# Two finished chunks copied out of their accumulator banks early, in a fused linear-attention and SoLU kernel

## The chip, the cores and the metric

The kernel runs on one core of a Trainium2 chip. The metric is the device time of one execution in microseconds (us). All data is float32 on the engines; the weights arrive as float64 and are converted on the chip. Five engines work in parallel, each through its own queue of instructions in order: TensorE (PE in the profile, with its weight loads as PEld), VectorE (DVE), ScalarE (ACT), GpSimd (POOL) and SyncE (SP), which here only issues DMAs. Matmul results land in PSUM banks, which the other engines read; a bank is written again only after its readers are done.

## The reference

The first half is a gated linear recurrence over 4 batches, 8 heads, 768 steps and a head dimension of 48. The second half takes its output, one row of 384 numbers for each of 3072 tokens, through a feed-forward block with a softmax-gated activation and a layer norm.

```python
for t in range(S):
    state = alpha[:, :, t, :, None] * state + einsum('bhd,bhde', k[:, :, t], v[:, :, t])
    y[:, :, t] = einsum('bhd,bhde->bhe', q[:, :, t], state)
x = y.transpose(0, 2, 1, 3).reshape(3072, 384)
h = x @ w_in                                  # 384 -> 1024
solu = h * softmax(h)
ln = (solu - mean(solu)) / sqrt(var(solu) + 1e-6) * g_ln
out = ln @ w_out                              # 1024 -> 384
```

## The kernel before

The 768 steps are cut into six groups of 128 steps. One group covers all four batches, so it makes four chunks of 128 tokens; chunk n belongs to group n // 4 and batch n % 4. The order of all work is written out by hand in `fast_path`: every engine gets its instructions in the order in which the code issues them.

Attention for a group g needs these steps. `alpha_T(g)` transposes the decay factors on DVE (L179 and L182, 128x1024 and 128x512) into the buffer `aT`, after GpSimd has cleared one column of it (L188). `scan_back` and `scan_on` run multiplicative scans over `aT` on DVE (L204). Keys and queries are scaled by the scans' results; for group 1 this is L762 and L783 on DVE, straight out of PSUM banks. `move_lasts` and `move_firsts` rearrange the queries by DMAs from SyncE's queue into `q64`, the first 2064 columns of a tile named `lot`. `decay(g)` multiplies the running state on GpSimd (L264). `scores(g, half)` computes key-query products on PE (L280) into the four banks a0 to a3, and `masked(half)` multiplies them by the causal mask on DVE (L291), four instructions of 128x512. `read_state` and `read_values` (L329) write the attention output into the same four banks, and ScalarE copies it to SBUF as `x` (L359).

The feed-forward of a group starts with eight up products (`up`, L390), each into one of two banks named h, followed by exp on ScalarE (L404), a product on DVE (L405) and a square on ScalarE (L406). `down(n, half)` accumulates chunk n's output in eight matmuls of 128x385 (L501); column 384 collects the sum that the mean needs. There are two banks for these results (`ps_o`), so chunk n + 2 writes where chunk n was. `finish(n)` turns the accumulated chunk into the output: three small steps on DVE (L519, L521, L524), for group 0 also a correction by the mean row over 128x384 (L528), a power on GpSimd (L532, called pow below), a scaling on ScalarE (L534) into `o_sb`, and a store from SyncE's queue (L535). `o_mean` and `o_sb` have two buffers each.

The change lies in the stretch in which the four chunks of group 0 are brought down while group 1's attention runs and group 2's begins. There the order of calls is: `down(0, 1)`, `mean(1)`, `alpha_over(1)` (a range test on ScalarE, L196), `load(alpha, an, 2)`, `load(q, qn, 2)`, `down(1, 1)`, `keys_back(1)` (transposes L299 and ScalarE copies L301, L306), a scan, `apart()` (ScalarE, L248), `move_lasts()`, `finish(0)`, two scans with their query products, `move_firsts()`, `down(2, 0)`, the first scores, `finish(1)`, `decay(1)`, `masked(0)`, `down(2, 1)`, the second scores, `masked(1)`, `finish(2)`, `alpha_T(2)`, and then `down(3, ...)`, the reads, `scan_back(2)`, `keys_T(2)`, `keys(2)` (GpSimd, L228) and `finish(3)`.

Of the kernel before, what the change touches and what calls it, by code (L numbers as in the profile page):

```python
# [9 lines left out]
FP = mybir.dt.float32  # L10
# [4 lines left out]
ALU = mybir.AluOpType  # L15
AX = mybir.AxisListType
P = 128
# [15 lines left out]
def fast_path(ctx, tc, q, k, v, alpha, moe_w_in, moe_w_out, moe_g_ln, out):  # L33
# [12 lines left out]
    nc = tc.nc  # L46
    B, H, S, D = q.shape
    NTOK, DM = out.shape
# [13 lines left out]
    def pool(name, bufs, **kw):  # L62
        return ctx.enter_context(tc.tile_pool(name=name, bufs=bufs, **kw))
# [3 lines left out]
    work = pool("work", 2)  # L67
# [20 lines left out]
    mean_sb = const.tile([P, DM], FP, name="mean_sb")  # L88
# [5 lines left out]
    sums = const.tile([P, N, 4], FP, name="sums")  # L94
# [14 lines left out]
    SW = P + 1  # L109
    lot = const.tile([P, 4 * 768], FP, name="lot")  # L110
# [16 lines left out]
    st = [dict() for _ in range(N)]  # L127
# [3 lines left out]
    def load(src, dst, g):  # L131
        t = slice(g * P, (g + 1) * P)
        for b in range(B):
            nc.sync.dma_start(
                out=dst[32 * b : 32 * b + 32].rearrange("t h u d -> t h (u d)"),
                in_=src[b, :, t, :].rearrange("h (t u) d -> t h (u d)", u=TQ),
            )
# [40 lines left out]
    def firsts(src, dst):  # L178
        nc.vector.transpose(out=dst.rearrange("p h (t u) -> p h u t", u=TQ), in_=src[:, :, :, 0:E0])  # L179

    def lasts(src, dst):
        nc.vector.transpose(  # L182
            out=dst.rearrange("p j (i t u) -> p u j i t", u=TQ, i=2),
            in_=src[:, :, :, E0:D].rearrange("p (j i) u d -> p u j i d", i=2),
        )

    def alpha_T(g):
        nc.gpsimd.memset(aT[:, :, 0:1], 0.0)  # L188
        firsts(an, aT[:, 0:H, 1:SW])
        lasts(an, aT[:, H:NB, 1:SW])  # L190

    def alpha_over(g):
        x = an.rearrange("p h u d -> p (h u d)")
        sq = one.tile([P, 768], FP, name="sq").bitcast(U8)[:, 0 : x.shape[1]]
        for i, sign in enumerate((1.0, -1.0)):
            nc.scalar.activation(  # L196
                out=sq, in_=x, func=AF.Relu, scale=sign, bias=mone, accum_out=over[:, g, i : i + 1]
            )
# [12 lines left out]
    def scan_on(g, i):  # L211
        part = slice(NP * i, NP * i + NP)
        s = seed[i % 2]
        if i == 2:
            nc.vector.tensor_copy(out=fend[:, g], in_=h4[:, :, 1])

        least = small.tile([P, NP, 1], FP, name="least")
        nc.vector.tensor_scalar(out=least, in0=h4[:, part, 1:2], scalar1=LEAST, scalar2=None, op0=ALU.max)  # L218
        nc.vector.reciprocal(out=s[:, :, 0:1], in_=least)
        scan(aT[:, part], aT[:, part], s, False)  # L220
# [9 lines left out]
    def move_lasts():  # L230

        for b in range(B):
            i, c = divmod(b, 2)
            for k in range(2):
                nc.sync.dma_start(out=q64[64 * i + E0 : 64 * i + 64, c, k::2], in_=qe[32 * b : 32 * b + 32])
# [32 lines left out]
    def quarter(b):  # L268
        return slice(32 * b, 32 * b + 32)

    def banks(name, shape, n=B):
        return [ps_a.tile([P] + shape, FP, tag=f"a{b}", name=f"{name}{b}") for b in range(n)]
# [15 lines left out]
    def masked(half, batches=range(B)):  # L288
        a = masks[half]
        for b in batches:  # L290
            nc.vector.tensor_tensor(  # L291
                out=sT[:, b, half * NP : half * NP + NP], in0=a[b], in1=mask[:, None, :].to_broadcast([P, NP, P]),
                op=ALU.mult,
            )

    def keys_back(g, t=None):
        t = t or banks("tp", [NP, P], 3)
        for j in range(NB):
            nc.tensor.transpose(out=t[j // NP][:, j % NP], in_=kT[:, j], identity=ident)  # L299
        for i in range(2):  # L300
            nc.scalar.copy(  # L301
                out=kg[:, :, NP * i : NP * i + NP, 0:E0].rearrange("p b j d -> p j b d"),
                in_=t[i].rearrange("p j (b d) -> p j b d", b=B),
            )
        for m in range(2):
            nc.scalar.copy(  # L306
                out=kg[:, :, m::2, E0 + E1 * m : D + E1 * m].rearrange("p b j d -> p j b d"),
                in_=t[2].rearrange("p j (b k d) -> p j b k d", b=B, k=2)[:, :, :, m],
            )
# [69 lines left out]
    def u_of(g, f):  # L379
        return slots[((0, 5, 4), (1, 2, 3))[g % 2][f // 3]][:, T4 * (f % 3) : T4 * (f % 3) + T4]  # L380
# [114 lines left out]
    def down(n, half, part=range(HF)):  # L495
        g, b = divmod(n, B)
        d = st[n]
        if half == 0 and 0 in part:
            d["o"] = ps_o.tile([P, 512], FP, tag="o", name="o")
        for f in (half * HF + i for i in part):  # L500
            nc.tensor.matmul(  # L501
                d["o"][:, 0 : DM + 1], lhsT=u_of(g, f)[:, b * P : b * P + P], rhs=w_out[:, f], start=(f == 0),
                stop=(f == FC - 1), skip_group_check=True,
            )

    def finish(n):
        g, b = divmod(n, B)
        d = st[n]
        s, o = sums[:, n], d["o"][:, 0:DM]
        t0 = b * S + g * P  # L510
        if g == G - 1:
            o_sb = work.tile([P, DM], FP, name="o_sb")
            r = gr[g]["r"][:, b : b + 1]
            nc.vector.tensor_scalar(out=o_sb[:, 0:P], in0=o[:, 0:P], scalar1=r, scalar2=None, op0=ALU.mult)  # L514
            nc.scalar.activation(out=o_sb[:, P:DM], in_=o[:, P:DM], func=AF.Copy, scale=r)  # L515
            nc.scalar.dma_start(out=out[t0 : t0 + P, :], in_=o_sb)
            d.clear()
            return
        nc.vector.tensor_copy(out=s[:, 0:1], in_=d["o"][:, DM : DM + 1])  # L519
        t = small.tile([P, 1], FP, name="t")  # L520
        nc.vector.scalar_tensor_tensor(  # L521
            out=t, in0=s[:, 0:1], scalar=-1.0 / DFF, in1=s[:, 0:1], op0=ALU.mult, op1=ALU.mult
        )
        nc.vector.tensor_tensor(out=s[:, 3:4], in0=t, in1=gr[g]["s"][:, b : b + 1], op=ALU.add)  # L524
        if g == 0:

            o = work.tile([P, DM], FP, name="o_mean")
            nc.vector.scalar_tensor_tensor(  # L528
                out=o, in0=mean_sb, scalar=s[:, 0:1], in1=d["o"][:, 0:DM], op0=ALU.mult, op1=ALU.add
            )  # L530
        r = small.tile([P, 1], FP, name="r")
        nc.gpsimd.tensor_tensor(out=r, in0=s[:, 3:4], in1=mhalf, op=ALU.pow)  # L532
        o_sb = work.tile([P, DM], FP, name="o_sb")
        nc.scalar.activation(out=o_sb, in_=o, func=AF.Copy, scale=r)  # L534
        nc.sync.dma_start(out=out[t0 : t0 + P, :], in_=o_sb)  # L535
        d.clear()
# [82 lines left out]
    def mean(half):  # L619


        m = ps_h.tile([P, 512], FP, tag="h", name="sums")[:, 0:DM]
        if half == 0:
            for f in range(FC):
                r = quarter(f % 4)
                nc.tensor.matmul(
                    m[r], lhsT=ones[:, 0:32], rhs=w_out[:, f, 0:DM], start=f < 4, stop=f >= FC - 4,
                    tile_position=(0, r.start), skip_group_check=True,
                )
            made["m"] = work.tile([P, DM], FP, name="o_mean")  # L630
            nc.scalar.mul(out=made["m"], in_=m, mul=-1.0 / (32 * DFF))
        else:
            nc.tensor.matmul(m, lhsT=ones, rhs=made["m"], start=True, stop=True)
            nc.scalar.copy(out=mean_sb, in_=m)
# [34 lines left out]
    def three(name, where):  # L669
        return [pool.tile([P, NP, P], FP, tag=tag, name=f"{name}{i}") for i, (pool, tag) in enumerate(where)]  # L670
# [18 lines left out]
    for i in (2, 0, 1):  # L689
        if i == 1:  # L690
# [3 lines left out]
            out=qe[:, :, 0:P] if i == 2 else qv[:, part, 0:P], in0=t[i], in1=aT[:, part, 1:SW], op=ALU.mult  # L694
# [68 lines left out]
    mean(0)  # L763
    down(0, 1)
    mean(1)
    alpha_over(1)
    load(alpha, an, 2)
    tq += three("tp_q2", [(ps_h, "h")])
    turned(qn, ends_q, tq, range(H, NB))
    load(q, qn, 2)  # L770
    down(1, 1)
    keys_back(1, three("tp", [(ps_a, "a2"), (ps_a, "a3"), (ps_h, "h")]))
    scan_on(1, 2)
    nc.vector.tensor_tensor(out=qe[:, :, 0:P], in0=tq[2], in1=aT[:, H:NB, 1:SW], op=ALU.mult)
    apart()
    ends_of_decay()
    move_lasts()
    finish(0)
    in_range(7)
    for i in range(2):  # L780
        scan_on(1, i)
# [2 lines left out]
    move_firsts()  # L784
    down(2, 0)
    scores(1, 0)
    finish(1)
    decay(1)
    masked(0)
    down(2, 1)  # L790
    scores(1, 1)
    masked(1)
    finish(2)
    alpha_T(2)
    down(3, 0)
    read_begin()
    read_state(0)
# [87 lines left out]
    for g in range(1, G + 1):  # L885
# [10 lines left out]
        for s in range(FC):  # L896
# [16 lines left out]
            if todo:  # L913
                n, half = todo.pop(0)
# [24 lines left out]
    def compare(out, x, bound, op):  # L939
# [6 lines left out]
        out=chunks[:, :, 2], in0=sums[:, :, 2], scalar=0.25, in1=sums[:, :, 3], op0=ALU.mult, op1=ALU.is_le  # L946
# [6 lines left out]
    else:  # L953
# [9 lines left out]
        out=bad, in0=all_ok[0:1, 0:1], scalar1=float(P * ends[-1]), scalar2=None, op0=ALU.is_lt  # L963
# [451 lines left out]
```

## Time and profile before

| what | value |
|---|---|
| median of 4 runs | 383.38 us (382.6 to 384.52) |
| the profiled execution | 382.77 us, its span 381.0 us |
| granted TensorE clock, mean of the span | 0.997 |
| PE busy | 363.2 us, 95% of the span |
| DVE busy | 250.9 us, 66% |
| ACT busy | 144.2 us, 38% |
| POOL busy | 112.0 us, 29% |
| between 80 and 120 us: PE busy | 36.81 of 40 us |
| between 80 and 120 us: DVE busy | 35.40 of 40 us |

All terms below are from the profiled execution, whose clock starts with the span. A row of the order of time gives the start, the length, the engine, the line, the operation, what it writes and reads, how many instructions are merged in it, and in brackets how long the engine stood idle before and who ended that.

### The profile page before, as it was taken

What the parts mean: (1) busy time and instruction counts of PE and PEld (TensorE: products, weight loads), DVE (VectorE), ACT (ScalarE), POOL (GpSimd) and SP (SyncE); (2) the same over time, 40 slices, a digit from 0 to 9 for tenths busy, and PEclk for the clock granted to TensorE, in tenths of its full rate; (3) what the DMA queues carried; (4) which work ended last, traced back from release to release, by engine and by line L of the source; (5) the groups of instructions that cost most, each with busy time, mean ns of one, the idle gap of its engine ahead of it and who ended that gap; (6) DMA issues with size and microseconds to landing.
All of it is one profiled execution on the core that took longest, in us unless ns stands there. A gap on an engine that the chain in (4) does not pass through costs nothing. (4 is left out here: it accounts for less than half of the span.)

```text
span 381.0 us, 10060 instructions
## 1 busy us (share of the span) xinstructions
PE 363.2 (95%) x4341; PEld 216.1 (57%) x4341; DVE 250.9 (66%) x413; ACT 144.2 (38%) x255; POOL 112.0 (29%) x122
## 2 busy tenths in 40 slices
PE   8789899988999999999999999999999999999994
PEld 8675335556754656555665555665556565555552
DVE  0999878996999779884665875666874414444500
ACT  2528566672155436143261152341241132322100
POOL 6000000000243990455210475111475211332200
PEclk9999999999999999999999999999999999999998
DMA  9992968139239612927042626004033000000011
GB/s 184 168 330 79 211 211 210 41 89 189 66 85 192 159 37 64 186 58 179 4 105 58 132 70 167 22 4 99 7 78 78 22 2 21 23 22 21 22 45 48
DMA packets 72438, 36.05 MB, mean 95 GB/s; under 512 B 48184, under 2 KB 69952, under 8 KB 72384
## 3 DMA queue, kind: packets, MB, share of 16 engines
q1 hardware_dynamic: 71360, 34.39, 38.4%
q10 hardware_dynamic: 1024, 0.92, 0.7%
q8 instruction: 36, 0.59, 0.7%
q14 instruction: 18, 0.15, 0.1%
HBM read 25.30 MB, written 4.72 MB: 79 GB/s over the span
## 5 line engine op out<-in xcount | busy, mean ns | idle before, releaser
L390 PE MATMUL h<-x,w_in 128*128 128x512 f32 x288 | 133.4, 601 | 3.9 <-DVE room L405 2.7
L501 PE MATMUL o<-w_out,room 128*128 128x385 f32 x384 | 133.6, 492 | 1.1 <-DVE least L218 1.1
L501 PEld LDWEIGHTS o<-w_out,room 128*128 128x128 f32 x384 | 71.1, 189 | 56.0 <-issue 14.9
L390 PEld LDWEIGHTS h<-x,w_in 128*128 128x128 f32 x288 | 52.4, 189 | 63.2 <-issue 47.5
L405 DVE TENSOR_TENSOR room<-h,e 128x512 f32<-128x512 f32 x40 | 27.6, 689 | 58.1 <-ACT e L404 58.1
L404 ACT ACTIVATE e<-h 128x512 f32<-128x512 f32 x40 | 23.8, 596 | 89.0 <-PE h L390 88.8
L421 POOL TENSOR_TENSOR p<-p,e 128x512 f32<-128x512 f32 x30 | 40.8, 1359 | 26.6 <-ACT e L404 26.1
L406 ACT ACTIVATE u<-room 128x512 f32<-128x512 f32 x40 | 25.2, 630 | 43.9 <-DVE room L405 43.9
L532 POOL TENSOR_TENSOR r<-sums,mhalf 128x1 f32<-128x1 f32 x20 | 12.5, 627 | 87.0 <-DVE sums L524 86.9
L291 DVE TENSOR_TENSOR sT<-a,mask 128x512 f32<-128x512 f32 x44 | 27.3, 683 | 14.2 <-PE a L280 14.2
L421 DVE TENSOR_TENSOR p<-p,u 128x512 f32<-128x512 f32 x30 | 24.2, 806 | 8.4 <-ACT u L406 8.4
L280 PE MATMUL a<-qv,kT 32*128 32x128 f32 x704 | 24.9, 278 | 3.9 <-DVE least L218 1.8
L280 PEld LDWEIGHTS a<-qv,kT 32*128 32x128 f32 x704 | 22.0, 186 | 10.9 <-POOL p L421 2.2
L204 DVE TENSOR_TENSOR_SCAN hT<-aT,unit 128x516 f32<-128x516 f32 x18 | 22.3, 1281 | 8.7 <-ACT aT L677 8.6
L204 DVE TENSOR_TENSOR_SCAN aT<-aT,seed 128x516 f32<-128x516 f32 x18 | 24.4, 1356 | 0.6
L329 PE MATMUL y<-sT,vn 128*32 128x128 f32 x768 | 22.9, 274 | 0.8 <-issue 0.4
L329 PEld LDWEIGHTS y<-sT,vn 128*32 128x32 f32 x768 | 20.8, 110 | 4.1 <-issue 3.4
L228 POOL TENSOR_TENSOR kT<-kT,hT 128x1024 f32<-128x1024 f32 (+1 forms) x8 | 13.3, 1681 | 28.8 <-DVE kT L179 28.8
L196 ACT ACTIVATE sq<-an,mone 128x1536 uint8<-128x1536 f32 x12 | 18.9, 1575 | 0.2
L534 ACT ACTIVATE o_sb<-o,r 128x384 f32<-128x384 f32 x16 | 9.3, 580 | 25.1 <-POOL r L532 25.1
L243 POOL COPY qe<-hT 128x4 f32<-128x4 f32 x5 | 1.0, 192 | 58.4 <-DVE hT L204 58.4
L359 ACT COPY x<-y 128x384 f32<-128x384 f32 x24 | 11.2, 478 | 14.6 <-PE y L329 14.4
(142 smaller groups left out, 367.6 us busy)
## 6 DMA issues: line engine op xcount, KB each, us to landing
vn<-in_v_dram SPq DMA_DIRECT2D x24, 192.0 KB, 4.7
an<-in_alpha_dram SPq DMA_DIRECT2D x20, 192.0 KB, 4.6
out_dram<-o_sb SPq DMA_DIRECT2D x20, 192.0 KB, 1.9
room<-in_moe_w_in_dram SPq DMA_DIRECT2D x6, 512.0 KB, 7.5
room<-in_moe_w_out_dram SPq DMA_DIRECT2D x8, 384.0 KB, 4.1
kn<-in_k_dram SPq DMA_DIRECT2D x16, 192.0 KB, 4.6
qn<-in_q_dram SPq DMA_DIRECT2D x16, 192.0 KB, 4.8
lot<-qe SPq DMA_DIRECT2D x40, 64.5 KB, 2.1
```

The lines of the kernel that those rows point to most:

```text
L196: nc.scalar.activation(out=sq, in_=x, func=AF.Relu, scale=sign, bias=mone, accum_out=over[:, g, i : i + 1])
L204: nc.vector.tensor_tensor_scan(out=o, data0=a, data1=s, initial=1.0, op0=ALU.mult, op1=ALU.add)
L228: nc.gpsimd.tensor_tensor(out=kT[:, part], in0=kT[:, part], in1=hk[:, part], op=ALU.mult)
L280: nc.tensor.matmul(a[b][:, i], lhsT=kT[quarter(b), kb], rhs=qv[quarter(b), qb, 0:P], start=kb == h, stop=kb != h, tile_position=(32 * b, 0 ...
L291: nc.vector.tensor_tensor(out=sT[:, b, half * NP : half * NP + NP], in0=a[b], in1=mask[:, None, :].to_broadcast([P, NP, P]), op=ALU.mult,)
L329: nc.tensor.matmul(y_bank(b)[quarter(r), a], lhsT=lhsT, rhs=rhs, start=(b, r) not in begun, stop=stop, tile_position=(row, 32 * r), skip_g ...
L390: nc.tensor.matmul(h, lhsT=w_in[:, a, f * P : (f + 1) * P], rhs=d["x"][:, a].rearrange("p b t -> p (b t)"), start=(a == 0), stop=(a == KC ...
L404: nc.scalar.activation(out=e, in_=h, func=AF.Exp)
L405: nc.vector.tensor_tensor(out=u, in0=h, in1=e, op=ALU.mult)
L406: nc.scalar.activation(out=u2, in_=u, func=AF.Square)
L421: eng.tensor_tensor(out=p, in0=d[0][i] if f == 1 else p, in1=d[f][i], op=ALU.add)
L501: nc.tensor.matmul(d["o"][:, 0 : DM + 1], lhsT=u_of(g, f)[:, b * P : b * P + P], rhs=w_out[:, f], start=(f == 0), stop=(f == FC - 1), skip ...
```

## The change

A new step `hold(n)` lets ScalarE copy the 385 accumulated columns of a chunk from its bank into `lot`, behind the columns that `q64` uses. It is called for chunks 0 and 1, right after `mean(1)` and after `down(1, 1)`. `finish(0)` and `finish(1)` read the copies instead of the banks. Both are called later: `finish(0)` after `masked(0)`, `finish(1)` after `masked(1)`. `alpha_T(2)` is called earlier, between `finish(0)` and the second half of the down product of chunk 2, so that DVE meets it between the two groups of masks. The stores of chunks 0 and 1 move with their finishes on SyncE's queue, and the power and the clearing of a column of `aT` come behind `decay(1)` on GpSimd's.

```diff
+    def hold(n):
+
+        a = 2 * H * SW + (DM + 1) * (n % 2)
+        st[n]["held"] = lot[:, a : a + DM + 1]
+        nc.scalar.copy(out=st[n]["held"], in_=st[n]["o"][:, 0 : DM + 1])
+
     def finish(n):
         g, b = divmod(n, B)
         d = st[n]
-        s, o = sums[:, n], d["o"][:, 0:DM]
+        s, whole = sums[:, n], d.get("held", d["o"])
+        o = whole[:, 0:DM]
...
-        nc.vector.tensor_copy(out=s[:, 0:1], in_=d["o"][:, DM : DM + 1])
+        nc.vector.tensor_copy(out=s[:, 0:1], in_=whole[:, DM : DM + 1])
...
-            o = work.tile([P, DM], FP, name="o_mean")
+            centred = work.tile([P, DM], FP, name="o_mean")
             nc.vector.scalar_tensor_tensor(
-                out=o, in0=mean_sb, scalar=s[:, 0:1], in1=d["o"][:, 0:DM], op0=ALU.mult, op1=ALU.add
-            )
+                out=centred, in0=mean_sb, scalar=s[:, 0:1], in1=o, op0=ALU.mult, op1=ALU.add
+            )
+            o = centred
...
     mean(1)
+    hold(0)
     alpha_over(1)
     load(alpha, an, 2)
...
     down(1, 1)
+    hold(1)
     keys_back(1, three("tp", [(ps_a, "a2"), (ps_a, "a3"), (ps_h, "h")]))
...
     move_lasts()
-    finish(0)
     in_range(7)
...
     down(2, 0)
     scores(1, 0)
-    finish(1)
     decay(1)
     masked(0)
+    finish(0)
+    alpha_T(2)
     down(2, 1)
     scores(1, 1)
     masked(1)
+    finish(1)
     finish(2)
-    alpha_T(2)
     down(3, 0)
```

## The prediction

> **What bounds the kernel now.** I read the first part of the page, then the order of time of TensorE (PE) from 82 us on, then VectorE (DVE) and GpSimd (POOL) over the same stretch, and last the DMA queue of SyncE. The page says which engine a saving has to reach:
>
> ```profile
> PE 363.2 (95%) x4341; PEld 216.1 (57%) x4341; DVE 250.9 (66%) x413; ACT 144.2 (38%) x255; POOL 112.0 (29%) x122
> ```
>
> PE is busy in nearly every slice, so the kernel gains only what PE's idle gaps lose. In PE's order of time (start, length, and in brackets the idle time before it and who ended it) those that the change can reach are:
>
> ```profile
> 83.97 2.83 PE L501 MATMUL o<-w_out,room 128*128 128x385 f32 x8 [1.14 <-DVE least L218]
> 88.45 2.06 PE L280 MATMUL a<-qv,kT 32*128 32x128 f32 x62 [1.24 <-DVE qv L783]
> 98.01 1.17 PE L329 MATMUL y<-lot,state 64*32 64x128 f32 x64
> 114.83 2.84 PE L390 MATMUL h<-x,w_in 128*128 128x512 f32 x6 [0.82 <-DVE room L405]
> 124.41 0.60 PE L280 MATMUL a<-qv,kT 32*128 32x128 f32 x8 [0.28 <-POOL qv L256]
> 125.34 2.01 PE L280 MATMUL a<-qv,kT 32*128 32x128 f32 x56 [0.32 <-ACT qv L248]
> ```
>
> Together 3.80 us. After 126 us PE has 0.11, 0.11 and 0.60 idle and then none that counts, so what is gained at 126 us stays. The first gap is the wait for a bank: L501 of chunk 2 writes where chunk 0's result stood, and finish(0) has to read it first (its L528 ends at 83.82; the profile names the instruction after it). The second is the score bank a1, which still holds queries until the second L783 has read it. The third row has no gap, and I will need it. VectorE:
>
> ```profile
> 82.75 0.15 DVE L519 COPY sums<-o 128x1 f32<-128x1 f32 x1
> 83.21 0.61 DVE L528 SCALAR_TENSOR_TENSOR o_mean<-mean_sb,sums,o 128x384 f32<-128x384 f32 x1
> 83.73 0.17 DVE L218 TENSOR_SCALAR least<-hT 128x4 f32<-128x4 f32 x1
> 90.36 2.49 DVE L291 TENSOR_TENSOR sT<-a,mask 128x512 f32<-128x512 f32 x4 [0.99 <-PE a L280]
> 95.31 2.48 DVE L291 TENSOR_TENSOR sT<-a,mask 128x512 f32<-128x512 f32 x4 [2.47 <-PE a L280]
> 98.73 2.06 DVE L179 STREAM_TRANSPOSE aT<-an 128x1024 f32<-128x1024 f32 x1
> 101.62 3.41 DVE L204 TENSOR_TENSOR_SCAN hT<-aT,unit 128x516 f32<-128x516 f32 x3
> ```
>
> finish(0) stands in front of the scans and queries that PE waits for; DVE then idles 0.99 + 2.47 = 3.46 us around the masks, and afterwards is behind until 124 us. POOL:
>
> ```profile
> 96.39 1.69 POOL L264 TENSOR_TENSOR state<-state,lot 128x384 f32<-128x384 f32 x2 [6.91 <-DMA lot<-qv]
> 107.14 3.32 POOL L228 TENSOR_TENSOR kT<-kT,hT 128x1024 f32<-128x1024 f32 x2 [8.15 <-DVE kT L179]
> ```
>
> The decay of the state (L264) waits for the moved queries and ends at 98.08, just as PE begins to read the state.
>
> **Step 1, the two copies.** No row has 128x385 from a bank to SBUF; the nearest are L634 and L359 at 0.48 us for 128x384, and after L634 the next instruction starts 0.37 later. I take 0.37 to 0.63 (the longest L534) for each, and 0.37 as what is added. hold(0) starts when mean_sb is done at 77.5, behind the end of down(0,1) at 76.4. It delays alpha_over by 0.37, and with it the loads of alpha and queries on SyncE, which wait for alpha_over (80.88 to 81.25). hold(1) needs down(1,1), over at 81.51, and is through by 82.0, when the key copies L301 start anyway (81.99, after 1.13 idle): nothing added. Were it 0.2 more, apart() at 83.47 would take it, and that is not needed before 85.7.
>
> **Step 2, finish(0) leaves the chain.** From L519 at 82.75 to L218 at 83.73 are 0.98 us. Without them every scan and query is 0.98 earlier: the second L783 ends at 87.41 and not 88.39. down(2,0) starts at 82.83, since its bank was emptied by ScalarE, and ends at 85.7; the scores wait for a1 still, and resume at 87.47. PE has gained 0.98; the rest of the two gaps (2.38) only moves together. finish(1) leaves DVE's path at no cost or gain: it lay in an idle stretch.
>
> **Step 3, what comes between the masks.** First masks 90.36 - 0.98 = 89.38; four masks take 2.40 to the next start (95.31 to 97.71), so finish(0) starts at 91.78, alpha_T(2) at 92.76, and with 2.89 for its two transposes (98.73 to 101.62) the second masks start at 95.65 and end at 98.13. Before they ended at 97.79. The scores for them end at 94.3, so they now wait for DVE. Their four banks are the ones that L329 at 98.01 writes, so PE, which comes there at 97.03, has to wait. It takes 16 passes (0.29 us) for the first two banks before it needs the fourth: that was at 98.30, and is now 98.13 and a signal, 98.18. **Of the 0.98 gained, 0.12 is left.** The alpha for these transposes had landed at 86.95, 0.37 later now: no wait.
>
> **Step 4, the decay.** On SyncE, chunk 0's output (issued at 91.84; with it the next move starts 0.67 later) no longer stands before the moves of the first dimensions. Against it the chain is 0.37 late. L264 so moves by -0.67 to +0.37; I take -0.3 and an end at 97.8, behind the masks. GpSimd's pow of finish(0) and the memset of aT now stand behind the decay: pow at 97.8 to 98.4, o_sb(0) until 99.0. finish(2) writes the o_mean buffer of chunk 0 at about 99.5, so it is just free; the first scan_back needs the memset at 98.5 and comes at 100. Third o_sb waits for the store of the first to land, 2.0 us after its issue, at about 101.5, and then the copies of x, due at 102.9, follow it on ScalarE: 0.8 us to spare.
>
> **Step 5, VectorE is ahead.** Its idle time falls from 3.46 to about 1.97 (87.41 to 89.38): scan_back(2) starts 1.5 us earlier, at 100.1. keys_T, and POOL's L228, move with it. finish(3), which stood behind L228 with its small steps (L521 1.33, L524 1.11 instead of 0.16), does so again 1.5 earlier; its bank is full at 107.05. L405 of the first up product moves from 114.11 to 112.6. The second L405 needs exp after PE's second up product, which is only 0.12 early, so there DVE's lead falls to about 1.35.
>
> **Step 6, PE's later gaps.** The h bank is free at 113.3, PE comes at 113.9: the gap of 0.82 goes (lead 0.94). The queries on POOL (L256, after DVE's L179) and apart() on ACT come 1.35 earlier: the gap of 0.28 goes, 0.32 shrinks to 0.25. Sum: 0.12 + 0.82 + 0.28 + 0.07 = **1.29 us**, and a lead of DVE smaller than 1.35 cuts it one for one.
>
> **A rule against the change.** L528 used to read one operand from a bank; for chunks 0 and 1 all now lie in SBUF. Rows on this: with both operands in SBUF, DVE's L421 after L524 starts 0.24 late while a pow runs, though the pow lasts 0.55:
>
> ```profile
> 299.79 0.69 DVE L421 TENSOR_TENSOR p<-p,u 128x512 f32<-128x512 f32 x1 [0.24 <-ACT u L406]
> 299.63 0.55 POOL L532 TENSOR_TENSOR r<-sums,mhalf 128x1 f32<-128x1 f32 x1 [7.20 <-DVE sums L524]
> ```
>
> By such rows finish(1) and finish(2) lose 0 to 0.5 together; I take 0.1, since the decay is over before finish(1) and the long step starts ahead of its own pow. The Trainium skill ("SBUF — State Buffer", section on the two separate sides) says that a VectorE operation with two SBUF inputs and a GpSimd operation that reads SBUF shut each other out for a whole instruction. Taken literally that would cost an estimated two pows of 0.55, and leave 0.2 us of the gain.
>
> **How the numbers stand.** The profiled run took 382.77 us for a span of 381.0; minus 1.29 is 381.48. The median of the runs shown is 383.38, 0.61 above it, so the forecast is 382.1. About 0.3%, 1.15 us, is what a measurement of this kernel can tell from no change; the line lies at 382.2.
>
> **Rivals.** *Swallowed*: DVE loses its lead to GpSimd and to longer transposes (L179 at 141.45 takes 2.24, L182 after it 1.22, so 0.2 more), and with a lead of 0.4 to 0.9 the kernel gains 0.3 to 0.8: 382.6 to 383.1. For it: steps of 0.16 have taken 1.33 beside L228. Against: POOL has only short work from 98 to 105. Chance 0.22.
> *Slower, by the moves of the queries*: read_state, pow(0), o_sb(0), finish(2) and scan_back now all hang on the decay. Up to a decay that ends at 98.2 it costs nothing; from there it eats DVE's lead of 1.5 and the gaps that PE would still have had, 1.42 together; from 99.7 on the kernel is slower than before, one us for each. One DMA issue of 0.59 that takes 2.57, as a key load at 112.84 does, puts the end at 99.8, about no change; two of them (the next such, a value load at 118.39, takes 2.36) put it at 101.6, 1.9 slower: 385.3. Against it: the moves overlap no other load once the queries have landed (90.5, now 90.9). Chance 0.13.
> *More*: the gap of 0.32 goes too and the masks are not late: 1.8 us, 381.6. Chance 0.05. That the copies do nothing is excluded: in the changed order the matmul after keys_back waits for ScalarE in place of VectorE.
> The forecast keeps 0.60, at 381.8 to 382.5; I count 0.50 of it beyond 0.3%. Faster: 0.50 + 0.05 = 0.55. Same: 0.10 + 0.22 = 0.32. Slower: 0.13. The range from 381.5 to 383.7 leaves out nearly all of the slower case and little else.
>
> **What would show it.** Right: no gap before L501 at 82.8; scores resuming at 87.5; a new gap of about 0.9 us at the first state read, ended by the masks; the 0.82 gap gone; scores of the next group about 1.3 earlier. Wrong: the state read released by GpSimd, or after 98.3; scan_back(2) later than 100.7; a gap left before the third up product.

## The result, and the profile after

The changed kernel takes 381.79 us in the median (380.58 to 383.92, 52 runs); beside it the kernel before took 383.12 (78 runs). The ratio is 0.9966, with a 95% interval of 0.9956 to 0.9976: a gain of 1.3 us or 0.34%. 382.1 was forecast. One run of the kernel before in a later set, 392.5 us at a mean clock of 0.948, is left out below.

The profiled execution of the changed kernel took 382.26 us, with a span of 380.5. Its start-up happened to run 0.70 us ahead of that of before, long before the change: the query transposes into `tp_q` (L164 of the second call), the last step that the change leaves alone, stand at 76.94 and at 77.64. I therefore count times **from there** and call them T; T 10 is 87.64 before and 86.94 after. The first part of the page:

```profile
PE 364.2 (96%) x4341; PEld 217.1 (57%) x4341; DVE 249.4 (66%) x413; ACT 145.0 (38%) x257; POOL 111.8 (29%) x122
```

ScalarE has the two copies more; TensorE is recorded as busy for 1.0 us longer with the same work. Its order of time says where:

```profile
81.95 2.76 PE L501 MATMUL o<-w_out,room 128*128 128x385 f32 x8
86.78 3.67 PE L280 MATMUL a<-qv,kT 32*128 32x128 f32 x62 [1.66 <-DVE qv L792]
97.96 1.90 PE L329 MATMUL y<-lot,state 64*32 64x128 f32 x64
111.72 5.42 PE L390 MATMUL h<-x,w_in 128*128 128x512 f32 x12
123.74 0.60 PE L280 MATMUL a<-qv,kT 32*128 32x128 f32 x8
124.67 2.01 PE L280 MATMUL a<-qv,kT 32*128 32x128 f32 x56 [0.32 <-ACT qv L248]
```

The 1.14 us before L501 is gone, the scores resume at T 9.85 instead of 10.81, and the gap of 0.82 before the third up product is gone (that product is now the second half of the row at 111.72). But one number is out of place: the same 62 passes of scores take **3.67 us, not 2.06**. The table by stretches shows why; its columns are busy time of PE, PEld, DVE, ACT and POOL, the granted TensorE clock, the DMA share and GB/s:

```profile
83.37:86.79 3.42, 1.76 (x8) 0.76 (x7) 3.22 (x6) 2.58 (x6) 0.00 (x0) 1.00 1.06 224
86.79:90.20 3.41, 3.41 (x62) 3.41 (x62) 0.00 (x0) 0.00 (x0) 0.00 (x0) 0.50 1.17 217
90.20:93.61 3.41, 3.41 (x27) 1.93 (x27) 3.32 (x9) 0.00 (x0) 0.00 (x0) 1.00 0.59 123
```

For exactly 3.41 us the clock was granted at half. That this begins as the scores resume is a coincidence of this execution; in the others below it begins up to 1.5 us after the wait. VectorE waits for those scores:

```profile
90.22 2.48 DVE L291 TENSOR_TENSOR sT<-a,mask 128x512 f32<-128x512 f32 x4 [3.49 <-PE a L280]
93.60 2.03 DVE L179 STREAM_TRANSPOSE aT<-an 128x1024 f32<-128x1024 f32 x1
96.42 2.46 DVE L291 TENSOR_TENSOR sT<-a,mask 128x512 f32<-128x512 f32 x4
100.75 3.47 DVE L204 TENSOR_TENSOR_SCAN hT<-aT,unit 128x516 f32<-128x516 f32 x3
```

so the first scan of group 2 starts at T 23.81, against 23.97 before. The lead of 1.5 us that the prediction built on is not there, and TensorE ends at T 298.49, where it ended before (298.46). GpSimd's rows are no longer the last ones to arrive:

```profile
95.16 1.65 POOL L264 TENSOR_TENSOR state<-state,lot 128x384 f32<-128x384 f32 x2 [15.76 <-DMA lot<-qv]
106.46 3.32 POOL L228 TENSOR_TENSOR kT<-kT,hT 128x1024 f32<-128x1024 f32 x2 [5.52 <-DVE kT L179]
```

The decay is over at T 19.87, 0.57 earlier than before, and TensorE comes to read the state at T 21.02, later than that. The read itself takes 1.90 us and not 1.17: its last banks wait for the second masks, which end at T 21.94. This is the new wait that the prediction's step 3 speaks of, but it stands inside a row and not in front of one. This execution has, from T on, **gained nothing**. The 1.3 us of the median must come from executions of another kind.

### The profile page after: what moved, and what is told of

It reads as the page before. It is cut to its first block, busy times and chain, and to the rows that moved or that the text cites. A ratio compares the mean times of both kernels' runs of the same rounds, so it can differ in the third digit from the quotient of the medians.

```text
span 380.5 us, 10059 instructions
## 1 busy us (share of the span) xinstructions
PE 364.2 (96%) x4341; PEld 217.1 (57%) x4341; DVE 249.4 (66%) x413; ACT 145.0 (38%) x257; POOL 111.8 (29%) x122
## 5 line engine op out<-in xcount | busy, mean ns | idle before, releaser
L501 PE MATMUL o<-w_out,room 128*128 128x385 f32 x384 | 133.5, 492 | 0.0
L501 PEld LDWEIGHTS o<-w_out,room 128*128 128x128 f32 x384 | 71.1, 189 | 54.7 <-issue 13.3
L280 PE MATMUL a<-qv,kT 32*128 32x128 f32 x704 | 26.5, 291 | 4.0 <-DVE least L218 1.7
L280 PEld LDWEIGHTS a<-qv,kT 32*128 32x128 f32 x704 | 23.6, 198 | 11.1 <-POOL p L421 2.2
L421 DVE TENSOR_TENSOR p<-p,u 128x512 f32<-128x512 f32 x30 | 23.4, 781 | 8.4 <-ACT u L406 8.4
```

The lines of the kernel that those rows point to most:

```text
L280: nc.tensor.matmul(a[b][:, i], lhsT=kT[quarter(b), kb], rhs=qv[quarter(b), qb, 0:P], start=kb == h, stop=kb != h, tile_position=(32 * b, 0 ...
L421: eng.tensor_tensor(out=p, in0=d[0][i] if f == 1 else p, in1=d[f][i], op=ALU.add)
L501: nc.tensor.matmul(d["o"][:, 0 : DM + 1], lhsT=u_of(g, f)[:, b * P : b * P + P], rhs=w_out[:, f], start=(f == 0), stop=(f == FC - 1), skip ...
```

## The experiments

### The parts of the change

Two kernels take the change apart at `alpha_T(2)`. The first is the changed kernel with only that call put back:

```diff
     finish(0)
-    alpha_T(2)
     down(2, 1)
...
     finish(2)
+    alpha_T(2)
     down(3, 0)
```

> The changed kernel with one part undone: alpha_T(2) stands behind finish(2) again, everything else as changed. Theory (VectorE's lead, cashed in at PE's later gaps, is the gain; the early 0.98 us is swallowed): VectorE idles again between the two groups of masks, scan_back(2) starts where it did before (within 0.2 us), PE reads the state about 0.7 us earlier and gives that back in a gap of about 1.5 us before the third up product; within 0.3 us of the kernel before, ratio 0.9995 to 1.0005, plus what a drop of the clock at the scores may add. Rival (the gain is finish(0) leaving the chain in front of PE): 0.7 to 1.0 us faster than before, as much as the whole change or nearly, ratio 0.9975 to 0.998.

Measured: ratio 1.0021 (0.9997 to 1.0044), median 384.29. scan_back(2) starts 1.6 later than before (T 25.52; the clock fell at the scores here too; 0.6 because the second masks end later and 1.0 because finish(1) now stands between them and `alpha_T(2)`). The lead at the first up product is lost, and TensorE waits for VectorE:

```profile
115.85 2.84 PE L390 MATMUL h<-x,w_in 128*128 128x512 f32 x6 [2.05 <-DVE room L405]
```

The rival (finish(0) leaving the chain is the gain) is out: the scores start 1.0 us earlier, and the kernel is no faster. Its three runs with a full clock, sorted below, stand at 383.11. With VectorE later than before, though, this kernel can't show what the early scores would bring by themselves.

The second is the kernel before with that one part:

```diff
     masked(0)
+    alpha_T(2)
     down(2, 1)
...
     finish(2)
-    alpha_T(2)
```

> The kernel before with one part alone: alpha_T(2) stands between the two groups of masks; no copies, finish(0) and finish(1) where they were. Theory: VectorE's idle 2.47 us is filled, scan_back(2) starts about 2.5 us earlier, the 0.82 and 0.28 us gaps go; 1.25 us faster than before, ratio 0.9967, as fast as the whole change. Rival (finish(0) leaving the chain is the gain): within 0.3 us of before, ratio 1.000.

Measured: 0.9943 (0.9920 to 0.9966), median 381.81. One moved call gives as much as the whole change; the interval's upper end, 0.9966, is the whole change's ratio. Its profiled execution kept the full clock:

```profile
84.54 2.83 PE L501 MATMUL o<-w_out,room 128*128 128x385 f32 x8 [1.14 <-DVE least L218]
89.01 2.06 PE L280 MATMUL a<-qv,kT 32*128 32x128 f32 x62 [1.23 <-DVE sums L519]
98.58 1.16 PE L329 MATMUL y<-lot,state 64*32 64x128 f32 x64
111.45 5.42 PE L390 MATMUL h<-x,w_in 128*128 128x512 f32 x12
123.43 0.60 PE L280 MATMUL a<-qv,kT 32*128 32x128 f32 x8
```

Both waits of before are still there (1.14 and 1.23), the state is read at the same T 20.37, and yet the scan starts at T 21.26 (2.71 earlier), the gap before the third up product is gone, and TensorE ends at T 296.89, 1.57 earlier than before.

The other half, the copies with both finishes left where they were:

```diff
     move_lasts()
+    finish(0)
     in_range(7)
...
     scores(1, 0)
+    finish(1)
     decay(1)
     masked(0)
-    finish(0)
-    alpha_T(2)
...
     masked(1)
-    finish(1)
     finish(2)
+    alpha_T(2)
```

> The changed kernel's copies alone: chunks 0 and 1 are copied out of their banks, but finish(0), finish(1) and alpha_T(2) stand where they stood before and finish reads the copies. Theory: the gap of 1.14 us before the down product of chunk 2 goes and the next one grows by as much, to 2.4 us, since the scores still wait for VectorE; within 0.2 us of before, ratio 1.000, unless the longer gap makes the clock drop, which would add up to 1.6 us in the executions that it falls in (ratio up to 1.004). Rival (the bank was what PE waited for): 1.0 us faster, ratio 0.9975.

Measured: 0.9995 (0.9973 to 1.0018), median 382.90. A bank freed early earns nothing: the wait moves to the scores, in pieces of 0.70 and 1.80. In the profile the clock then fell to half (89.37 to 92.79) and the down product behind the scores took 4.09 instead of 2.86.

### Both finishes before the first masks

VectorE waits for the scores anyway, so both finishes fit in there:

```diff
     scores(1, 0)
+    finish(0)
+    finish(1)
     decay(1)
     masked(0)
-    finish(0)
     alpha_T(2)
...
     masked(1)
-    finish(1)
     finish(2)
```

> The changed kernel with finish(0) and finish(1) both in front of the first masks (in the stretch in which VectorE waits for the scores) and alpha_T(2) alone between the masks. Theory: the second masks end at about 97.2 us on the clock of the profile before and no longer hold PE at the state read, where it keeps about 0.7 us; VectorE's lead at scan_back(2) grows to about 3.5 us; all of the 1.42 us of later gaps but little goes: 1.8 to 2.1 us faster than before, ratio 0.995, about 0.6 us better than the change. Rival (the early part is the whole gain): like the change, ratio 0.9966.

Measured: 0.9939 (0.9916 to 0.9962), median 381.64, although the clock fell twice in its profiled execution, once before the stretch of the change (20.56 to 23.98) and once at the scores (88.83 to 92.24; 3.69 for the 62 passes). With that fall it still ends at T 297.85, 0.2 to 0.7 before the four profiled executions of the changed kernel (298.02 to 298.52), which all have one: the second masks are over at T 20.84 and not at 21.43 to 21.94. Whether it is 0.6 better than the change, as expected, stays open: the two were not run side by side, and their medians, 381.64 and 381.79, are close.

### The clock

Each timed run comes with its mean granted clock. One fall of 3.41 us to half, in a span of 380, lowers it by 0.0045. The mean falls a little too when the clock goes down behind TensorE's last matmul, which costs no time: in the fourteen profiled executions this takes 0.000 to 0.004 off. So a run without a fall lies at 0.9965 or more, one with a fall at 0.992 to 0.996 (three profiled executions with just one fall in TensorE's work have a mean of 0.992), and 0.991 or less means two. At the borders single runs can be in the wrong class. All sets of runs together, median of each class:

| kernel | runs | clock 0.9965 and more | one fall | two or more (0.991 and less) |
|---|---|---|---|---|
| before | 77 | 52 at 382.77 | 25 at 384.03 | none |
| the change | 78 | 36 at 381.12 | 29 at 382.27 | 13 at 383.70 |
| alpha_T(2) alone | 18 | 15 at 381.45 | 3 at 382.36 | none |
| the change without its alpha_T(2) | 12 | 3 at 383.11 | 5 at 384.23 | 4 at 385.52 |
| copies alone | 12 | 8 at 382.69 | 3 at 384.09 | 1 at 386.70 |
| both finishes first | 8 | 3 at 380.66 | 3 at 381.84 | 2 at 383.08 |
| the change with five matmuls of ones (below) | 12 | 4 at 382.21 | 8 at 383.52 | none |
| both finishes first with them (below) | 12 | 6 at 381.64 | 6 at 383.18 | none |
| filled (below) | 13 | 9 at 380.16 | 4 at 381.52 | none |

(54 runs of the change are from the first set, two more than its median counts, and 24 from the two sets below.) From class to class the medians rise by 0.9 to 1.5 us, where three runs or more stand on either side. With a full clock the change is worth **1.65 us** (382.77 - 381.12; within the two later sets alone 1.5 and 2.1); but 42 of its 78 runs have a fall, against 25 of 77 before, and that brings the difference of the medians down to 1.3.

The control, and two kernels with matmuls that keep TensorE busy while it waits:

> The changed kernel itself, as the control of the two that follow. Theory (VectorE's lead is the gain; and the wait of 1.6 us before the scores, now in one piece, lets the granted clock fall to half for 3.4 us in part of the executions, at about 1.5 us each): executions whose mean clock is 0.997 or more at about 381.2 us, those at 0.993 to 0.996 about 1.2 to 1.5 us above, those under 0.993 about 2.5 us above. Rival (the half clock is an accident of the one profiled execution): no such steps; about 30 in 100 executions at any clock.

Measured: 0.9978 (0.9960 to 0.9997), median 382.19; three runs with a full clock at 381.2 to 381.7, six with one fall at 380.7 to 382.7, three with two at 383.3 to 383.8. The steps are there, but the expectation had one border wrong: its last class, under 0.993, mixes one fall and two, and three of its six runs are only about 1 us above the full clock. In the profile the clock fell at the scores once more (87.24, after a wait of 1.61).

```diff
     down(2, 0)
+    warm(5, ps_h, "h")
     scores(1, 0)
```

> The changed kernel with five matmuls of ones (128x128, into a free h bank) put before the first scores of group 1, where TensorE waits for VectorE; they write nothing that is read. Theory: they take about 1.2 us of the wait of 1.66 us, the clock does not fall at the scores, and hardly any execution has a mean clock under 0.993; the median is 0.4 to 0.8 us below the control's, at about 0.9960 of before. Rival (the fall does not come from the wait): the same share of executions at low clocks and the same median, or 0.1 to 0.3 us more.

Measured: 0.9991 (0.9974 to 1.0008), median 383.03: the expectation failed, but not as the rival had it. The order of time says what happened:

```profile
84.94 1.28 PE L446 MATMUL warm<-ones 128*128 128x128 f32 x10
87.09 2.06 PE L280 MATMUL a<-qv,kT 32*128 32x128 f32 x62 [0.45 <-DVE qv L792]
98.05 0.55 PE L329 MATMUL y<-lot,state 64*32 64x128 f32 x16 [1.33 <-POOL state L264]
98.85 1.02 PE L329 MATMUL y<-lot,state 64*32 64x128 f32 x48 [0.25 <-POOL state L264]
```

The scores ran at full clock, in 2.06. TensorE came to the state read early, waited 1.33 + 0.25 there, and **the clock fell at 100.02**, 1.2 us behind that wait. Four runs have a full clock, and at 382.21 they too are 1.1 us above those of the change; so the later fall is not all that these matmuls cost. GpSimd's decay was late too: it ended at T 21.47, a full 1.03 after that of before. The last two moves of queries had been issued by T 16.92, as in the changed kernel, and landed at T 19.66 and 19.97 instead of 18.06 and 18.80. A move lands in sixteen parts, and only the last of them is late: the fifteenth came at T 18.11 and 18.73. Among these moves lies a transfer that is not the kernel's, in the DMA view of the stretch from 94 to 96 us (queue and kind: packets, MB, share of 16 engines):

```profile
q8 instruction: 1, 0.02, 4.1%
```

It is 16 KB of instructions at T 17.0, taking 1.3 us; in the changed kernel it comes at T 21.4, after the moves. That TensorE was further on by then is the likely reason, but no run shows it.

The same matmuls in the variant with both finishes first:

> The variant with finish(0) and finish(1) in front of the first masks and alpha_T(2) between the masks, with the five matmuls of ones before the scores. Theory: 2.1 us below before without a fall of the clock, and few executions have one; ratio 0.994 to 0.995, 0.6 us better than the changed kernel with the five matmuls. Rival (VectorE's lead has no more to give): as the changed kernel with the five matmuls.

Measured: 0.9982 (0.9963 to 1.0002), median 381.87. The expectation failed: half of the runs have a fall, and the kernel is not faster than without these matmuls (381.64, in another set). Against the changed kernel with them (383.03) it gains 1.2 us in the median, which speaks against the rival. Here too the fetch came at T 16.9, the moves landed at T 19.14 and 19.40, again by one part of sixteen, and the decay ended at T 20.94. In the twelve other profiled executions no fetch of this size comes between T 13.0 and 19.6, and the decay starts at T 17.5 to 19.2 instead of 19.8 and 19.3. That the fetch delays the moves is so read from profiles; no run isolated it.

### Filling the waits with the kernel's own work

```diff
     down(2, 0)
+    down(2, 1)
     scores(1, 0)
+    finish(0)
+    finish(1)
     decay(1)
     masked(0)
-    finish(0)
     alpha_T(2)
-    down(2, 1)
+    down(3, 0)
     scores(1, 1)
     masked(1)
-    finish(1)
     finish(2)
-    down(3, 0)
+    down(3, 1, (0, 1))
     read_begin()
     read_state(0)
-    down(3, 1, (0, 1))
     read_state(1)
```

> The variant with finish(0) and finish(1) in front of the first masks, and TensorE's waits filled with the kernel's own work: the second half of chunk 2's down product stands before the first scores, the first half of chunk 3's before the second scores, and two more of its matmuls before the state is read. Theory: no wait before the scores, so no fall of the clock there; a wait of about 1.4 us stays at the state read, behind the second masks, but TensorE is 1.6 us ahead after it; the later gaps go as far as VectorE's lead of about 2.5 us reaches; 2.2 to 2.4 us below before, ratio 0.994. Rival (the scores, 0.9 us later, hold VectorE back as much as TensorE gains): 1.2 to 1.5 us below before, ratio 0.9965.

Measured: 0.9946 (0.9924 to 0.9968), median 380.55. No fall from 5.8 us to TensorE's last matmul:

```profile
82.67 5.35 PE L501 MATMUL o<-w_out,room 128*128 128x385 f32 x16
87.95 2.07 PE L280 MATMUL a<-qv,kT 32*128 32x128 f32 x64
96.85 2.70 PE L329 MATMUL y<-lot,state 64*32 64x128 f32 x125 [0.55 <-POOL state L264]
```

The wait before the scores is gone, the one at the state read is 0.55, and TensorE ends at T 295.59, 2.87 before the kernel before. The rival's ratio, 0.9965, still lies within the interval; the second set of runs, below, leaves it outside.

### A last comparison on one chip

The changed kernel in two sets, and the two variants that avoid the long wait:

> The changed kernel again, for a profiled execution in which the clock does not fall at the first scores, and for a comparison on one chip with the two that follow. Theory: where the clock stays full, the second masks end about 20.4 us after the query transposes (97.6 to 98.2 on the profile before's clock), the first scan of group 2 starts 1.3 to 1.6 us earlier than before, PE has a wait of about 1 us at the state read, and PE comes to the end 1.5 us earlier than before. Where it falls again at the first scores, PE ends about where the kernel before ends, within 0.3 us. Over the timed executions: 0.9966 of before. Rival (the early 0.98 us survives to the end): with a full clock no wait at the state read, and 2.3 us earlier at the end.

> A second look at the changed kernel, with the same expectations as for the look before it: with a full clock 1.5 us earlier at the end, with a fall at the first scores within 0.3 us of the kernel before.

Measured: 0.9964 (0.9943 to 0.9986), median 381.62, and a single further run at 382.62. The clock fell in both profiled executions (87.49 and 87.17), and TensorE ended at T 298.02 and 298.52, against 298.46: within 0.45 of before, where 0.3 was expected. So all four profiled executions of the changed kernel had the fall at the scores, and none shows it with a full clock; that half of the expectation stays untested in a profile, and rests on the timed runs.

> alpha_T(2) between the masks as the only part, beside the whole change on one chip. Theory: same gain with a full clock (1.55 us), but TensorE's waits before the scores stay in two pieces of 1.14 and 1.23 us, so that fewer executions have a fallen clock: none or one in ten under 0.9925, where the whole change has a quarter; median 0.2 to 0.6 us below that of the whole change. Rival (the copies add to the gain): 0.3 us or more above the whole change.

Measured: 0.9968 (0.9951 to 0.9986), median 381.65, level with the whole change (381.62) and not 0.2 to 0.6 below it. Runs with a full clock: ten of twelve at 381.40, against six of twelve at 380.72 for the change. With a full clock the change is so 0.7 us lower than `alpha_T(2)` alone here, and 0.3 over all sets, which is more than expected; its more frequent falls (six of twelve against two) are what that is lost through.

> The variant without a wait before the scores, beside the whole change on one chip. Theory: 2.6 us below before with a full clock and none under 0.9925; median about 1.5 us below that of the whole change, ratio to before 0.9935 to 0.9955.

Measured: 0.9931 (0.9910 to 0.9951), median 380.80; none at 0.9925 or below. It is 0.8 us below the changed kernel in the median, not 1.5, with six runs against twelve whose ranges overlap. TensorE ends 2.2 us earlier than before in its profiled execution. It beats the kernel before clearly.

## Why the prediction was right, point by point

**Step 1** held. The copies took 0.49 and 0.48, the first added 0.37, the loads of alpha were issued 0.38 later (T 3.62 for 3.24), the key copies were not moved.

**Step 2** held: the scores resume 0.96 to 1.04 earlier in four profiles, 0.98 was the sum.

**Step 3** held in kind. In the run with the five matmuls, the only profile with the change's three parts and a full clock up to the state read, TensorE comes there at T 19.39 (the prediction's 97.03 is T 19.39) and the second masks end at T 20.29 (20.49); but there it was the late decay that released the read. In the four profiles of the changed kernel the masks did hold it, 0.3 to 0.7 us inside the read (1.43 to 1.90 instead of 1.17), with TensorE's arrival and the end of the masks 0.9 to 1.6 us later than forecast, behind the half clock. No profile shows the change's early 0.98 being swallowed at the masks with a full clock. That it does not bring its own gain to the end is shown from the other side, by the runs without `alpha_T(2)`, where TensorE gives it back before the third up product.

**Step 4** was mis-sized. The decay ended at T 19.18 to 19.96 in four profiles of the changed kernel, 0.5 to 1.3 earlier than before where 0.3 was taken, and 1.03 later with the five matmuls; both go outside the range of -0.67 to +0.37. The issues of the moves alone, which the term was made of, ended at T 16.20 to 17.01, and with the five matmuls at 16.92: the issues do not tell when the moves land. The chain of the slower rival exists: in that run finish(2) waited 0.18 for o_sb(0), and pow(0) started only at T 21.42. It decided nothing in the changed kernel itself.

**Step 5** is the step that carries the gain, and the size of the lead was the wrong part: 0.16 to 0.67 us in the profiled executions, not 1.5, because the masks wait for scores at half clock. With the five matmuls and a full clock at the scores it was 0.78, cut by the late decay. With `alpha_T(2)` alone and a full clock the lead was 2.71.

**Step 6** was right in kind, and small. The gap of 0.82 went; of the 0.28 there were 0.11 to 0.30 left in the four profiles of the changed kernel, and 0.32 stayed. But from the first up product to the third TensorE takes 6.84 us and not 7.82, so that gap was worth 0.98, and with `alpha_T(2)` alone the first up product came 0.30 earlier, with no gap in the profile before it. The idle time recorded for the modelled TensorE was so smaller than what the waits cost: 0.98 + 0.30 + 0.28 is 1.56, and TensorE ended 1.57 earlier there.

**The rule that speaks against the change** (the Trainium skill, "SBUF — State Buffer", the two separate sides) was rightly not taken at two whole pows. The four steps of finish(1) and of finish(2) take 0.97 and 0.98 between them as before, and it is GpSimd's pow that waits, recorded with 0.86 instead of 0.55. But it shows itself in a trace: where the decay was late, one step of finish(1), 0.16 by itself, took 0.77 beside it:

```profile
98.05 0.77 DVE L531 TENSOR_TENSOR sums<-t,s 128x1 f32<-128x1 f32 x1
97.15 1.64 POOL L264 TENSOR_TENSOR state<-state,lot 128x384 f32<-128x384 f32 x2 [17.46 <-DMA lot<-qv]
```

**The signs** that the prediction named are mixed. No gap is left before L501, the scores resume when it said, and the gap of 0.82 is gone. But two of its signs of being wrong stand in all four profiled executions of the changed kernel: the state is read after 98.3, which is T 20.66 (T 20.93 to 21.02), and scan_back(2) starts later than 100.7, which is T 23.06 (T 23.30 to 23.81). The scores of the next group, forecast 1.3 earlier, come 0.44 earlier to 0.06 later. In the run with the five matmuls GpSimd released the state read, another such sign. The later half of the path that the prediction drew, VectorE's lead and the gaps that it fills, is seen only with `alpha_T(2)` alone (next scores 1.55 earlier); for the changed kernel it rests on the timed runs with a full clock.

**What was missed** altogether is the clock. The prediction said that the rest of the two gaps "only moves together" and gave that no price. Two waits of 1.14 and 1.24 became one of 1.6, and after one of 1.6 the clock fell in all four profiles. The forecast of 382.1 against 381.79 is so right with the help of luck: 1.29 was put for a gain of 1.65 with a full clock, nothing for falls that take back 0.3 of it, and the two errors offset each other. Nearly all of the 0.3 that is left between 382.1 and 381.79 is the lower median of before (383.12, not 383.38).

## What to carry to other kernels

Work moved out of a chain in front of the bottleneck engine gains only if the next thing that it waits for moves as well; here one call put into an idle stretch of the engine that was behind later gave the whole gain of the median by itself. When several short waits are merged into one, look at the granted clock in the next stretch, and fill the wait with work that is needed anyway rather than with idle matmuls, which here carried the wait to the next place. A single profiled execution can show none of a gain that many timed runs have: sort the runs by their clock before explaining a trace.

## What was not expected of the hardware

A wait of TensorE of 1.58 to 1.80 us in this stretch was followed by 3.41 us of half clock in all eight profiled executions that had one (four of the changed kernel, one without `alpha_T(2)`, one with the copies alone, one with both finishes first, one at the state read), and waits of 1.0 to 1.24 never. (Where the falls of the 25 timed runs of the kernel before lie is not known.) The falls start a whole number of stretches of 3.41 us after the clock came up at the start (81.92 = 24 x 3.413 later in six of the eight). The Trainium skill ("TensorE: Matmul & The Clock Gate", What's actually happening) has such a free-running window of 3413 ns and lets the clock fall after a whole idle window; here half a window was enough.

The length of the wait alone does not decide, though: 2.05 us in the kernel without `alpha_T(2)` was not followed by a fall (a boundary of the stretches cut it into 0.66 and 1.40). What sorts the cases from 80 us on is the share of such a stretch in which a matmul of TensorE is recorded. It was 0.47 to 0.54 in the eight stretches that came before a fall, and 0.59 or more in all other stretches at full clock, up to TensorE's last. In the kernel before the two waits of 1.14 and 1.24 lie in two stretches, with 0.67 in each. Near the start, with narrower matmuls, the border lies elsewhere. Ahead of the first scores a wait of 1.80 us, which no boundary cut, was not followed by a fall in the kernel before, and one of 2.23 us in the kernel with both finishes first was:

```profile
19.64 2.08 PE L280 MATMUL a<-qv,kT 32*128 32x128 f32 x64 [1.80 <-DVE least L218]
19.85 3.20 PE L280 MATMUL a<-qv,kT 32*128 32x128 f32 x64 [2.23 <-DVE least L218]
```

The shares of those stretches were 0.47 and 0.35, and seven profiled executions, that one of before among them, had 0.47 to 0.54 there without a fall. What counts as activity stays open.
